# Sixteen instructions of batches 1 and 2 moved from VectorE to ScalarE in a fused attention + Fourier-mixing kernel

## The chip, the cores and the metric

The kernel runs on one core of a Trainium2 chip. The metric is the device time of one execution, in microseconds (us); lower is better. Engines are written as in the profile: PE is the matrix engine, PEld its weight loads, DVE is VectorE, ACT is ScalarE, POOL is GpSimd, SP issues most DMAs. L309 is line 309 of the kernel before.

## The reference

Four batches, each of 8 heads, 768 positions and 64 values per head. Stage one is block-sparse causal attention: a query sees its own block of 64 keys and the three blocks with the highest gate score (query times block mean of the keys). Stage two works on the 768 x 512 result `x` of each batch:

```python
mixed = real(fft(fft(x, axis=1), axis=2))
u = x + mixed
un = (u - mean(u)) / sqrt(var(u) + 1e-6)        # per row of 512
out = u + maximum(un @ w_ch1, 0) @ w_ch2        # 512 -> 2048 -> 512
```

## The kernel before, in words

Attention goes over 16 head pairs (`kk` = 0 to 15, four to a batch). For a pair, `stage_A` (L262) transposes k and q on PE into tiles `tp`; ACT casts the k parts to `kI` (L309), four casts to a pair, and DVE sums blocks into `kr` (L290). From pair 8 on, q is split into a high and a low half: ACT writes `qh` (L285) and DVE `ql` (L286). `stage_B` and `stage_C` compute gate scores and the mask, which DVE copies into `qg` (L355). `stage_S` (L374) makes scores `sc` in six sections to a pair; ACT's exp (L389) writes each to `ptl`, and from pair 7 on DVE masks the diagonal after the third section (L395). `stage_AV` (L397) multiplies with v into `av`, and DVE normalises into `x` (L415, L416).

A batch's Fourier part starts when its last pair is done:

- `stage_S1` (L463), twice (dt = 1, 0): sine sums `za` and cosine sums `ya` on PE. Each is evicted twice, in natural order (`zT`, `yT`, L487) and reversed (`zR`, `yR`, L489). DVE evicts z, ACT evicts y.
- `stage_S2` (L493), six row blocks (kt = 0 to 5): `mx` on PE, then `u` (L516) and row statistics (L518, L519) on DVE.
- `stage_N` (L523), once: a chain of small DVE instructions that ends in `rstd` and `nmr` (L543), then the normed rows `x`, six blocks: even ones on DVE (L546), odd ones on ACT (L550).
- `stage_T` (L553), six blocks: PE transposes a normed block into `unt` (L559), and it is evicted into `unT`: on DVE (L564), but the odd blocks of batch 0 on ACT (L562).
- `stage_M1` (L567), 16 units: `ha` and `hb` on PE (L575), ReLU to `hT` on ACT (L578) and DVE (L580). `stage_M2` (L583), 24 units of four matmuls (L589) into `ch`; after four units DVE adds `u` (L592) and SP stores.

The order on PE and POOL is written out by hand. The main loop (L713 to L747) emits attention of pair `kk`, and between its pieces `filler` takes units from a feed: `chain` holds the Fourier units of the batch just finished, `bulk` the M1 and M2 units of the batch before. A chain unit may go once a planned time (`feed.now`, costs of L597) has passed its predecessor by a gap (L603 to L605); until then bulk units go. So batch 1's Fourier part runs among batch 0's M2 units and the attention of pairs 8 to 10, and batch 2's among batch 1's M2 units and pairs 12 to 14. The order on the other engines is made by a scheduler; each engine runs its own list strictly in order.

Results of PE go to two pools: `sc` has 2 buffers (L380), everything else (`tp`, `av`, `mx`, `unt`, `ch`, `ha`, `hb`, `gt`, `za`, `ya`) shares 4 buffers of the tag `ps` (L152, L157). The scheduler picks which buffer a new tile takes, and the first matmul into it waits until the old tile's last reader is done.

Of the kernel before, what the change touches and what calls it, by code (L numbers as in the profile page):

```python
# [118 lines left out]
def kernel(  # L119
# [9 lines left out]
    nc = tc.nc  # L129
    B, H, S, D = q.shape  # L130
# [64 lines left out]


    LATE = 6


    SPLIT = 8  # L200
# [61 lines left out]
    def stage_A(kk, who, g):  # L262
# [18 lines left out]
        if who == 0:  # L281
            if kk < SPLIT:
                (nc.scalar.copy if kk == LATE else nc.vector.tensor_copy)(out=d["qt"][:, cols], in_=flat)
            else:
                nc.scalar.activation(out=d["qh"][:, cols], in_=flat, func=AF.Copy, scale=QS)  # L285
                STT(out=d["ql"][:, cols], in0=flat, scalar=QS, in1=d["qh"][:, cols], op0=MULT, op1=SUB)  # L286
            if g == 1 and kk != LATE:
                cast_q(kk)
# [174 lines left out]
    def stage_S1(b, dt):  # L463
        x = X[b]
        yps = pst([128, 2, KM], f"ya_{b}_{dt}")
        zps = pst([128, 2, KM], f"za_{b}_{dt}")


        if b == 0:
            zin, yin = ((ft[2], ft[0]), (ft[3], fc[1])) if dt == 1 else ((ft[2], fo[0]), (ft[3], ft[1]))  # L470
        else:
            zin, yin = (fo[dt],), (fc[dt],)
        for r in range(2):
            ops = [(x_[:, HST * r + t, :], ss_sb[:, t, r, :]) for x_ in zin for t in range(HST)]
            if dt == 0:
                ops += [(xmid[:, r, t, :], cs_sb[:, t, r, :]) for t in range(HST)]
            for n, (x_, w_) in enumerate(ops):
                nc.tensor.matmul(zps[:, r, :], x_, w_, start=(n == 0), stop=(n == len(ops) - 1))  # L478
        for r in range(2):
            ops = [(x_[:, HST * r + t, :], cs_sb[:, t, r, :]) for x_ in yin for t in range(HST)]  # L480
            for n, (x_, w_) in enumerate(ops):
                nc.tensor.matmul(yps[:, r, :], x_, w_, start=(n == 0), stop=(n == len(ops) - 1))
        for n, ps, cp in (("z", zps, nc.vector.tensor_copy), ("y", yps, nc.scalar.copy)):
            t0 = bpool.tile([128, KM, 2], F16, tag=f"{n}T", name=f"{n}T_{b}_{dt}", bufs=2)

            t1 = bpool.tile([128, KM - 1, 2], F16, tag=f"{n}R", name=f"{n}R_{b}_{dt}", bufs=2)
            cp(out=t0.rearrange("p m r -> p r m"), in_=ps)  # L487
            back = ps.rearrange("p r m -> p (r m)")[:, 1:KH - 1]
            cp(out=t1.rearrange("p m r -> p r m"),  # L489
               in_=back.rearrange("p (r m) -> p r m", r=2)[:, :, ::-1])  # L490
            x[n, dt] = (t0.rearrange("p m r -> p (m r)"), t1.rearrange("p m r -> p (m r)"))

    def stage_S2(b, kt):  # L493
        x = X[b]
        if kt == 0:
            x["u"] = bpool.tile([128, NST, DM], FP, tag="u_b", name=f"u_{b}", bufs=2)
            x["stat"] = spool.tile([128, NST, 2], FP, tag="stat6", name=f"stat6_{b}", bufs=2)
        u_b = x["u"]
        mps = pst([128, DM], f"mx_{b}_{kt}")
        hi = kt // HST  # L500
        ksl = slice(128 * (kt - HST * hi), 128 * (kt - HST * hi + 1))
        sd = sdp_sb if hi else sdn_sb
        for dt in range(2):
            half = mps[:, HD * dt:HD * (dt + 1)]
            nc.tensor.matmul(half, x["y", dt][hi][:, ksl], cd_sb[:, dt, :], start=(dt == 0), stop=False)  # L505
            nc.tensor.matmul(half, x["z", dt][hi][:, ksl], sd[:, dt, :], start=False,  # L506
                             stop=(dt == 1 and b > 0))
        split = dict(m=HD, r=2)
        xv = x["x"][:, kt, :].rearrange("p (m r) -> p m r", **split)
        uv = u_b[:, kt, :].rearrange("p (m r) -> p m r", **split)  # L510
        mv = mps.rearrange("p (r m) -> p m r", **split)
        if b == 0:
            nc.tensor.matmul(mps, id16, xv.rearrange("p m r -> p r m"), start=False, stop=True)
            nc.scalar.copy(out=uv, in_=mv)  # L514
        else:
            nc.vector.tensor_tensor(out=uv, in0=mv, in1=xv, op=ADD)  # L516
        bst = spool.tile([128, 6], FP, tag="bst", name=f"bst_{b}_{kt}")
        nc.vector.bn_stats(out=bst, in_=u_b[:, kt, :])  # L518
        nc.vector.bn_aggr(out=x["stat"][:, kt, :], in_=bst)  # L519
        if kt == NST - 1:  # L520
            stage_N(b)

    def stage_N(b):  # L523
        x = X[b]
        I32 = mybir.dt.int32
        stat = x["stat"]

        def small(n, dtype=FP):
            return spool.tile([128, NST], dtype, tag=n, name=f"{n}_{b}", bufs=2)

        rstd, nmr = small("rstd6"), small("nmr6")
        vr, yi, t2 = small("vr"), small("yi", I32), small("t2")
        ve = nc.vector
        ve.tensor_scalar(out=vr, in0=stat[:, :, 1], scalar1=1e-6, scalar2=None, op0=ADD)
        ve.tensor_scalar(out=yi, in0=vr.bitcast(I32), scalar1=1,
                         scalar2=None, op0=mybir.AluOpType.arith_shift_right)
        ve.tensor_scalar(out=yi, in0=yi, scalar1=-1, scalar2=0x5f3759df, op0=MULT, op1=ADD)
        y0 = yi.bitcast(FP)
        for _it in range(2):
            STT(out=t2, in0=y0, scalar=-0.5, in1=y0, op0=MULT, op1=MULT)  # L540
            ve.tensor_tensor(out=t2, in0=t2, in1=vr, op=MULT)
            STT(out=(rstd if _it == 1 else y0), in0=t2, scalar=1.5, in1=y0, op0=ADD, op1=MULT)
        STT(out=nmr, in0=stat[:, :, 0], scalar=-1.0, in1=rstd, op0=MULT, op1=MULT)  # L543
        for st in range(NST):
            if st % 2 == 0:
                nc.vector.tensor_scalar(out=x["x"][:, st, :], in0=x["u"][:, st, :],  # L546
                                        scalar1=stat[:, st, 0:1], scalar2=rstd[:, st:st + 1],
                                        op0=SUB, op1=MULT)
            else:
                nc.scalar.activation(out=x["x"][:, st, :], in_=x["u"][:, st, :], func=AF.Identity,  # L550
                                     scale=rstd[:, st:st + 1], bias=nmr[:, st:st + 1])

    def stage_T(b, st):  # L553
        x = X[b]
        if st == 0:
            x["unT"] = bpool.tile([128, NDT, S], F16, tag="unT", name=f"unT_{b}")
        tps = pst([128, NDT, 128], f"unt_{b}_{st}", dtype=F16)
        for dt in range(NDT):
            nc.tensor.transpose(tps[:, dt, :], x["x"][:, st, 128 * dt:128 * (dt + 1)], id16)  # L559
        dst = x["unT"][:, :, 128 * st:128 * (st + 1)]  # L560
        if b == 0 and st % 2 == 1:
            nc.scalar.copy(out=dst, in_=tps)  # L562
        else:
            nc.vector.tensor_copy(out=dst, in_=tps)  # L564
# [32 lines left out]
    M1_COST, M2_COST, S1_COST, S2_COST, T_COST = 1.3, 0.87, 1.3, 0.5, 0.43  # L597

    def queue_batch(b, start):
        last = start  # L600
        units = []

        s1_gap = 6.0 if b else 3.5  # L603
        s2_gap = 1.8 if 0 < b < B - 1 else 1.0
        t_gap = {0: 4.0, B - 1: 6.0}.get(b, 7.5)  # L605
        for dt in (1, 0):
            last = Unit(lambda dt=dt: stage_S1(b, dt), S1_COST, last, s1_gap if dt == 1 else 0.0)
            units.append(last)
        for kt in range(NST):
            last = Unit(lambda kt=kt: stage_S2(b, kt), S2_COST, last, 2.5 if kt == 0 else s2_gap)  # L610
            units.append(last)
        for st in range(NST):
            last = Unit(lambda st=st: stage_T(b, st), T_COST, last, t_gap if st == 0 else 0.2,
                        allowed=(lambda: b == 0 or m1_left[b - 1] == 0))
            units.append(last)

        def arm():
            def m1(it):
                stage_M1(b, it)
                m1_left[b] -= 1  # L620
            for it in range(NIT):
                feed.bulk.append(Unit(lambda it=it: m1(it), M1_COST))
            for st in range(NST):
                for part in range(4):
                    feed.bulk.append(Unit(lambda st=st, part=part: stage_M2(b, st, part), M2_COST))

        units.append(Unit(arm, 0.0, last, 0.8))
        feed.chain.extend(units)
# [19 lines left out]
    def main(fn, cost, *a):  # L648
        fn(*a)
        feed.spend(cost)  # L650
# [6 lines left out]
    with tc.manual_schedule(engines={mybir.EngineType.PE, mybir.EngineType.Pool}):  # L657
# [55 lines left out]
        for kk in range(NK):  # L713
            for p in range(6):
# [9 lines left out]
                if p == 2:  # L724
                    if kk + 2 < NK:
                        main(stage_AA, 0.7, kk + 2, 0)
                        if kk + 2 != LATE:
                            cast_v(kk + 2)
# [61 lines left out]
```

## Time and profile before

| | |
|---|---|
| median of 3 runs | 334.54 us (333.73 to 336.84) |
| profiled execution | 334.11 us, span 332.3 us, mean granted PE clock 0.99 |
| DVE busy | 236.8 us, 71% |
| ACT busy | 180.3 us, 54% |
| POOL busy | 83.8 us, 25% |
| ACT `x` L550, 128x512 (x12) | 804 ns each |
| DVE `x` L546, 128x512 (x12) | 542 ns each |
| ACT `unT` L562, 128x512 (x3) | 579 ns each |
| DVE `unT` L564, 128x512 (x21) | 419 ns each |
| ACT `yR` L489, 128x384 (x8) | 591 ns each |
| DVE `zR` L489, 128x384 (x8) | 572 ns each |

How to read it: all times come from one profiled execution, which took 334.11 us as a whole; the 1.81 us beyond the span lie around the program. A line of the timeline gives start, duration, engine, source line, operation, output<-input, shape, count, and in brackets the engine's idle time before it with what ended it. A row of several instructions is drawn from the first start to the last end, so neighbouring instructions overlap a little. PE records overlap as well (a 128x512 matmul is drawn with 379 ns, while 96 of them in a row take 20.73 us, 216 ns each), so what PE loses is read from the starts.

### The profile page before, as it was taken

To read this page: it belongs to the slowest core of one execution; us is meant where nothing else is said; L and a number is where in the kernel's file an instruction comes from. 1 tells how busy PE (TensorE), PEld (TensorE's weight loads), DVE (VectorE), ACT (ScalarE), POOL (GpSimd) and SP (SyncE) were. 2 spreads that over 40 slices of the span, in tenths; PEclk is the share of its full clock that TensorE was granted. 3 is DMA by queue.
4 is the path that set the end of the run, shared out by engine and by line. 5 is a ranking of instruction groups with operands and counts; after the bars stand their busy time and mean duration, and the time that the engine had idled before them with its cause. 6 is when DMAs were issued, how large, how long until landed. Compare 5 with 4: busy or idle time off the path is not lost.

```text
span 332.3 us, 7010 instructions
## 1 busy us (share of the span) xinstructions
PE 312.6 (94%) x2712; PEld 203.5 (61%) x2712; DVE 236.8 (71%) x750; ACT 180.3 (54%) x276; POOL 83.8 (25%) x137
## 2 busy tenths in 40 slices
PE   8799998995999989998999989999999999999995
PEld 3567776884766665565665666655666654556442
DVE  3877889689766898999666897998557588433211
ACT  3178889787876855438386854535764302244000
POOL 8545573452452030503132040502030000000000
PEclk9999999998799999999999999999999999999999
DMA  8999989995599341334424001010000011100021
GB/s 191 233 225 214 251 136 218 158 204 119 82 185 155 72 97 52 91 98 112 129 47 97 2 0 35 32 65 32 34 0 2 2 64 63 65 1 2 32 95 63
DMA packets 85312, 31.18 MB, mean 94 GB/s; under 512 B 77736, under 2 KB 81136, under 8 KB 85280
## 3 DMA queue, kind: packets, MB, share of 16 engines
q1 hardware_dynamic: 79984, 25.88, 31.2%
q0 software_dynamic: 3552, 4.40, 8.5%
q10 hardware_dynamic: 1744, 0.46, 0.6%
q8 instruction: 21, 0.34, 0.5%
q14 instruction: 11, 0.09, 0.1%
HBM read 28.63 MB, written 6.29 MB: 105 GB/s over the span
## 4 chain that ended last, share of the span: by engine, by line
PE 73%; DVE 16%; ACT 6%; DMA 1%; issue 1%; POOL 1%; ACTq 0%; DVEq 0%
PE ch L589 22%; PE ha L575 14%; PE sc L384 8%; PE hb L575 7%; PE av L410 5%; ACT kI L309 3%; PE g L321 3%; DVE mx L338 2%; PE za L478 2%; DVE ptl L395 2%; ACT ptl L389 2%; PE tp L277 2%; PE gt L352 2%; PE mx L505 2%; DVE kr L290 2%; PE mx L506 2%
## 5 line engine op out<-in xcount | busy, mean ns | idle before, releaser
L389 ACT ACTIVATE ptl<-sc 128x896 f16<-128x896 f32 x96 | 87.4, 918 | 46.5 <-PE sc L384 36.6
L589 PE MATMUL ch<-w_sb,hT 128*128 128x512 f16 x384 | 91.4, 379 | 0.5 <-DVE qT L286 0.5
L575 PEld LDWEIGHTS <-w_sb 128*128 128x128 f16 x512 | 48.8, 97 | 38.2 <-issue 4.3
L575 PE MATMUL ha<-unT,w_sb 128*128 128x512 f16 x256 | 65.7, 379 | 1.6 <-DVE hT L580 0.7
L384 PE MATMUL sc<-qg,kI 76*128 76x512 f16 (+3 forms) x256 | 55.7, 309 | 3.4 <-ACT ptl L389 3.4
L589 PEld LDWEIGHTS <-hT 128*128 128x128 f16 x384 | 36.2, 97 | 35.1 <-issue 0.6
L578 ACT ACTIVATE hT<-ha 128x512 f16<-128x512 f32 x64 | 38.1, 597 | 32.2 <-PE ha L575 32.1
L580 DVE TENSOR_SCALAR hT<-hb 128x256 f16<-128x256 f32 x64 | 26.8, 421 | 29.7 <-PE hb L575 29.5
L575 PE MATMUL hb<-unT,w_sb 128*128 128x256 f16 x256 | 38.4, 272 | 1.1 <-ACT hT L578 0.7
L427 POOL TENSOR_TENSOR fs<-x 128x384 f16<-128x384 f16 x12 | 10.9, 908 | 109.0 <-DVE x L416 88.5
L384 PEld LDWEIGHTS <-kI 76*128 76x128 f16 x256 | 24.2, 100 | 20.1 <-issue 3.1
L309 ACT CAST kI<-tp 64x384 f16<-64x384 f32 x57 | 27.0, 473 | 14.6 <-DVE kr L290 13.6
L592 DVE TENSOR_TENSOR u<-ch,u 128x512 f32<-128x512 f32 x24 | 16.5, 686 | 19.9 <-PE ch L589 19.6
L410 PE MATMUL av<-v,ptl 128*128 128x65 f16 x672 | 26.2, 195 | 0.0
L410 PEld LDWEIGHTS <-ptl 128*128 128x128 f16 x672 | 24.8, 98 | 1.9
L290 DVE TENSOR_REDUCE kr<-tp 128x6 f32<-128x384 f32 x32 | 17.2, 548 | 5.3 <-PE tp L277 5.3
L395 DVE TENSOR_TENSOR ptl<-ptl,ut 128x384 f16<-128x384 f16 x36 | 15.9, 479 | 6.0 <-ACT ptl L389 5.7
L550 ACT ACTIVATE x<-u,nmr,rstd 128x512 f16<-128x512 f32 x12 | 8.9, 804 | 19.0 <-DVE nmr L543 19.0
L388 PE MATMUL sc<-ltri,id 128*128 128x128 f16 x84 | 18.8, 224 | 0.0
L416 DVE TENSOR_TENSOR x<-av,rcp 128x384 f16<-128x384 f32 x32 | 17.8, 557 | 0.9
L518 DVE BATCH_NORM_STATS2 bst<-u 128x6 f32<-128x512 f32 x24 | 16.6, 692 | 1.2 <-ACT u L514 0.7
L355 DVE COPY qg<-gt 12x640 f16<-12x640 f16 x32 | 15.5, 484 | 1.8 <-PE gt L352 1.0
(112 smaller groups left out, 423.1 us busy)
## 6 DMA issues: line engine op xcount, KB each, us to landing
vn<-in_v_dram SPq DMA_DIRECT2D x32, 192.0 KB, 3.3
out_dram<-u SPq DMA_DIRECT2D x24, 256.0 KB, 2.0
kn<-in_k_dram SPq DMA_DIRECT2D x30, 192.0 KB, 3.5
qn<-in_q_dram SPq DMA_DIRECT2D x30, 192.0 KB, 3.4
w_sb<-in_moe_w_ch_dram POOLq DMA_DIRECT2D x8, 256.0 KB, 7.1
w_sb<-in_moe_w_ch_dram POOLq DMA_DIRECT2D x4, 512.0 KB, 8.2
cs_sb<-c_CS SPq DMA_DIRECT2D x1, 289.5 KB, 5.0
ss_sb<-c_SS SPq DMA_DIRECT2D x1, 289.5 KB, 5.3
```

The lines of the kernel that those rows point to most:

```text
L290: nc.vector.tensor_reduce(out=d["kr12"][:, 6 * g:6 * g + 6], in_=ps.rearrange("p a (x c) -> p a x c", x=2), axis=mybir.AxisListType.X, op=ADD)
L309: nc.scalar.copy(out=dst, in_=src_)
L384: nc.tensor.matmul(sp[:, co:co + (a1 - a0)], d["kI"][e][0:76, 128 * jt:128 * (jt + 1)], d["qg"][e][0:76, a0:a1], start=True, stop=not diag)
L388: nc.tensor.matmul(sp[:, co:co + 128], id16, ltri, start=False, stop=True)
L389: nc.scalar.activation(out=pt[:, SEC * s:SEC * (s + 1)], in_=sp[:, 0:SEC], func=AF.Exp, scale=0.125 if kk < SPLIT else 0.125 / QS)
L395: nc.vector.tensor_tensor(out=dg, in0=dg, in1=um, op=MULT)
L410: nc.tensor.matmul(av[:, st, 0:65], pt[:, o:o + 128], d["v16"][:, e, jt, 0:65], start=(cnt == 0), stop=(cnt == 20))
L416: nc.vector.tensor_tensor(out=x_b[:, :, 64 * h:64 * h + 64], in0=av[:, :, 0:64], in1=rcp.to_broadcast([128, NST, 64]), op=MULT)
L575: nc.tensor.matmul(hp_, w1_sb[:, dt, 128 * it:128 * (it + 1)], unT[:, dt, c0:c1], start=(dt == 0), stop=(dt == NDT - 1))
L578: nc.scalar.activation(out=hT[:, c0:c1], in_=hp_, func=AF.Relu)
L580: nc.vector.tensor_scalar(out=hT[:, c0:c1], in0=hp_, scalar1=0.0, scalar2=None, op0=mybir.AluOpType.max)
L589: nc.tensor.matmul(cps, x["hT"][it][:, 128 * st:128 * (st + 1)], w2_sb[:, it, :], start=(it == 0), stop=(it == NIT - 1))
```

## The change

A new name `BUSY` stands for batches 1 and 2. For these: the reversed casts `zR` go to ACT; all six normed blocks go to ACT; the odd `unT` evictions go to ACT. The gap before the first `stage_S2` unit is 3.5 in place of 2.5. Batches 0 and 3 are untouched (in batch 0 the odd `unT` evictions were on ACT already).

```diff
+    BUSY = range(1, B - 1)
...
-            cp(out=t1.rearrange("p m r -> p r m"),
+            (nc.scalar.copy if b in BUSY else cp)(out=t1.rearrange("p m r -> p r m"),
                in_=back.rearrange("p (r m) -> p r m", r=2)[:, :, ::-1])
...
         for st in range(NST):
-            if st % 2 == 0:
+            if st % 2 == 0 and b not in BUSY:
                 nc.vector.tensor_scalar(out=x["x"][:, st, :], in0=x["u"][:, st, :],
...
-        if b == 0 and st % 2 == 1:
+        if b < B - 1 and st % 2 == 1:
             nc.scalar.copy(out=dst, in_=tps)
...
-        s2_gap = 1.8 if 0 < b < B - 1 else 1.0
+        s2_gap = 1.8 if b in BUSY else 1.0
...
-            last = Unit(lambda kt=kt: stage_S2(b, kt), S2_COST, last, 2.5 if kt == 0 else s2_gap)
+            last = Unit(lambda kt=kt: stage_S2(b, kt), S2_COST, last, (3.5 if b in BUSY else 2.5) if kt == 0 else s2_gap)
```

In the built programs the lists of POOL are the same. ACT has 16 instructions more, DVE 16 fewer. On PE one thing moves: in batch 2, one unit of four `ch` matmuls stands ahead of the first `mx` unit in place of behind it. On SP one output store and one load of q change places. What PE's matmuls wait for changes around the transposes, since the scheduler hands out the `ps` buffers differently.

## The prediction

> **What bounds the kernel now.** I read the busy table first, then what PE waited for, then the timeline of all engines around the two places where the normed blocks are made, and last the granted clock around PE's one long stall.
>
> ```profile
> PE 312.6 (94%) x2712; PEld 203.5 (61%) x2712; DVE 236.8 (71%) x750; ACT 180.3 (54%) x276; POOL 83.8 (25%) x137
> ```
>
> PE is the bound, with 312.6 of 332.3 us. So an instruction moved between DVE and ACT is worth only what it takes from, or adds to, PE's waits. Counted from the starts of PE's instructions (each start against the usual step behind such an instruction), PE loses about 7 us in all between 119 and 262 us, where the Fourier parts of batches 1 and 2 lie. Most of it has causes that the change doesn't touch (0.8 at 119.20 and 1.2 at 196.43 behind ReLUs of DVE, 0.35 at 175.26). The waits near the change are these:
>
> ```profile
> PE unt L559 <- DVE x L416: 0.7, 1, 0.7
> ...
> PE ch L589 <- DVE qT L286: 0.5, 1, 0.5
> ```
>
> Both lie in batch 1's normed blocks. From the starts they cost PE 0.84 and 0.69 us. With the 0.49 us that the fourth `mx` of batch 1 waited at 138.20 for DVE's L286, 2.0 us is all that a lighter DVE could give back.
>
> The timeline of batch 1, of ACT, DVE and PE:
>
> ```profile
> 150.28 1.46 DVE L546 TENSOR_SCALAR x<-u,stat,rstd 128x512 f16<-128x512 f32 x3
> 150.43 2.22 ACT L550 ACTIVATE x<-u,nmr,rstd 128x512 f16<-128x512 f32 x3
> ...
> 152.67 1.46 ACT L309 CAST kI<-tp 64x384 f16<-64x384 f32 x3
> ...
> 153.20 0.38 PE L559 MATMUL unt<-id,x 128*128 128x128 f16 x4 [0.67 <-DVE x L416]
> ...
> 154.15 1.73 ACT L389 ACTIVATE ptl<-sc 128x896 f16<-128x896 f32 x2
> ...
> 155.76 0.55 PE L384 MATMUL sc<-qg,kI 76*128 76x512 f16 x3
> ...
> 157.06 1.02 PE L589 MATMUL ch<-w_sb,hT 128*128 128x512 f16 x4 [0.53 <-DVE qT L286]
> ```
>
> ACT works here without a pause: norms, casts, exps, each starting as the one before ends. In the program the first `unt` takes the buffer of a `tp` whose reader is the first of those casts, which ends near 153.15; the L416 that the bracket names ends at nearly the same time. PE already waits for ACT's list, not for DVE's sum. Batch 2:
>
> ```profile
> 224.46 2.22 ACT L550 ACTIVATE x<-u,nmr,rstd 128x512 f16<-128x512 f32 x3 [0.54 <-DVE nmr L543]
> ...
> 226.59 0.90 ACT L389 ACTIVATE ptl<-sc 128x896 f16<-128x896 f32 x1
> ...
> 228.03 0.92 ACT L389 ACTIVATE ptl<-sc 128x896 f16<-128x896 f32 x1 [0.55 <-PE sc L384]
> ...
> 230.00 0.55 PE L384 MATMUL sc<-qg,kI 76*128 76x512 f16 x3
> ```
>
> Here no casts of k stand in the list, ACT has pauses, and PE loses nothing.
>
> **The change part by part.** In all DVE is freed of 4 x 0.572 + 6 x 0.542 + 6 x 0.419 = 8.1 us, and ACT takes 4 x 0.591 + 6 x 0.804 + 6 x 0.579 = 10.7 us. Neither is on the path by itself.
>
> *Reversed casts, 4.* ACT's casts there start 0.45 us apart (122.19, 122.65). In batch 1 the second new cast stands ahead of the exp at 125.61, which so starts 0.45 later. DVE sat idle for 1.30 us until 126.57, waiting for that exp: the 1.1 us it was freed of go into that idle, and its mask starts 0.45 later. It then works on without idle to 135.15, where 0.28 of idle absorb that much. About 0.2 us reach the L286 that `mx` waits for at 138.20. Cost 0.2; bounds 0 (an idle I don't see) and 0.9 (both casts in full). In batch 2 the exp at 201.97 is 0.1 later, DVE again only idles (1.41 us before 202.91), and no PE wait follows it. Nothing; without that cover 0.45.
>
> *Gap of 3.5.* One unit of four `ch` matmuls (0.86 us) changes places with one `mx` unit in batch 2. The work is the same, and PE lost nothing there. Nothing; if the first `mx` were now the late one, its 0.43 us. The SP swap is two issues of about 0.4 us, of a q that pair 14 needs far later. Nothing.
>
> *Normed blocks and evictions, batch 1.* Six blocks on ACT: three take 2.22, one 0.80, so each further one 0.71; the six end at 150.43 + 0.80 + 5 x 0.71 = 154.78 instead of 152.65. Everything behind them on ACT is 2.13 later. Queued there are three casts to `kI`, two exps, two L285, an exp. Now PE, step by step:
> - First `unt`: takes the buffer of `av`, freed by L416, which DVE reaches earlier without its blocks (near 152.45). Starts near 152.5 in place of 153.20: 0.7 won.
> - Second `unt` waits for the eviction of the first (0.42 on DVE): 153.4. Then `ch`, 0.86.
> - q transposes take the buffer of the cast that now ends at 155.27: start 155.3, before 154.88.
> - Third `unt` takes the buffer of the last cast, 154.78 + 1.46 = 156.26: 156.3, before 155.54.
> - Score section at 155.76 needs the first exp's buffer: 156.28 + 0.92 = 157.20. Start 157.25, 1.5 later.
> - The `ch` of 157.06 takes the buffer of the second `unt`, which ACT evicts behind both exps: 156.28 + 1.73 + 0.58 = 158.6. 1.5 later.
> - ACT's L285, behind that eviction, then DVE's L286: the `gt` and `unt` at 158.01 and 158.41 go near 159.7 and 160.2.
>
> From there ACT has pauses (2.63 us before 160.09, 2.05 before 163.06), and the remaining `unT` fit in them. PE stays 1.75 us late. Bounds: 1.1, if L285 and L286 follow closer than I laid them; 2.1, the whole delay of ACT. I take 1.75, since the exp and the eviction alone make 1.5.
>
> *Batch 2.* The six end at 224.46 + 4.35 = 228.8, the two exps at 229.8 and 230.7. The score section of 230.00 finds its buffer free by 0.2. The sixth `unt` (232.57) waits for an eviction on ACT that stands behind one more exp: 230.7 + 0.58 + 0.9 + 0.58 = 232.8. Cost 0.3; bounds 0 and 1.75 (batch 1's). DVE's freed 1.45 us meet no PE wait.
>
> Sum: 0.2 + 1.75 + 0.3 = 2.25 us, on the profiled execution's 334.11: 336.4. That execution is 0.43 under the median of its three runs, so the sum is a little low if the next runs lie like that median.
>
> *The clock.* PE's granted clock fell once in this trace:
>
> ```profile
> 78.00:80.00 2.00, 0.43 (x5) 0.24 (x3) 1.90 (x6) 1.61 (x3) 1.23 (x2) 1.00 0.48 110
> 80.00:82.00 2.00, 0.52 (x4) 0.34 (x4) 1.93 (x6) 0.94 (x2) 0.54 (x1) 0.59 0.82 186
> ```
>
> (PE busy, PEld, DVE, ACT, POOL, clock.) PE was idle from 78.43 to 81.48; the clock went to half at 80.37, after 1.94 us of that idle, and stayed there for 6.83 us. By the same grid of 3.41 us, the stretch before the fall held 23% of matmul time (by starts, 216 ns to 512 columns), and the emptiest ones that kept their clock about 50%. My waits in batch 1 leave the idlest 3.41 us with some 44%, most of it transposes. So the row allows a fall without showing one: 0 to 3.4 us (half of 6.83). I take 0, since 44 is nearer to 50 than to 23. The Trainium skill ("TensorE: Matmul & The Clock Gate", rules for kernel authors) asks for no idle gaps over about 3 us between bursts; by it gaps of 0.3 to 0.9 us cost nothing and the sum stands. The trace is stricter, since the clock fell with 1.94 us of the gap behind it.
>
> **The rivals.**
> - *A lighter DVE pays (faster, or not slower).* PE's waits at 138.20, 153.20 and 157.06 vanish and ACT's list doesn't reach PE: 334.1 - 2.0 = 332.1, or with only part of it up to 334.8. For it: DVE is over 90% busy in 140 to 160, ACT 54% over all. Against: ACT has no pause from 150.06 to 157.46, and the exps wait behind the norms. It decides if the casts and exps that PE needs stand ahead of the added blocks; in the built list they stand behind.
> - *Batch 2 goes like batch 1.* If the score section of 230.00 misses its 0.2 us of margin and the waits chain, 1.75 in place of 0.3: 337.8. For it: the margin is small. Against: no casts there.
> - *The clock falls in batch 1.* 336.4 + 3.4 = 339.8. For it: the idle pieces lie close together. Against: no single one is over 0.9 us.
> - That the change does nothing at all would be 334.1, and falls under the first.
>
> **How the numbers follow.** Chances: the sum 0.56, with a range of its own of 335.0 to 337.4 (bounds of batch 1, and 0.3 to either side for the rest); DVE pays 0.16; batch 2 like batch 1 0.14; clock 0.14. A measurement of this kernel can tell about 1% from no change, 3.3 us: faster is under 331.2, slower over 337.9. Faster: 0.03, the far end of the first rival. Slower: the clock's 0.14, half of batch 2's, and a tail of the sum: 0.25. Same: 0.72. The range goes from 333.6 (upper half of the first rival) to 339.0 (batch 2 in full, and a part of a clock loss), and leaves out some 2 in 10.
>
> **What would show it.** After: six L550 in a row of about 4.35 us in each batch; the L309 and L389 behind them in batch 1 later by 2.1; PE waits of L277, L559, L384 and L589 between 153 and 160 us on ACT, 3 us in all, in place of 1.5; almost none in batch 2; the mask after batch 1's casts 0.45 later, its DVE idle longer. I am wrong if PE waits less around batch 1's transposes than before, if the six blocks take less than 4 us, or if the clock row has a second fall.

## The result and the profile after

The changed kernel takes 336.54 us (median of 18 runs, 335.81 to 339.18) against 334.43 us for the kernel before (18 runs, 333.29 to 336.86): ratio 1.0066, 95% interval 1.0049 to 1.0083, so about 2.2 us slower, under what counts as a difference here. The prediction was 336.4 us. The profiled execution took 336.49 us, its span is 334.7 us (before: 334.11 and 332.3).

In some executions of any of these kernels (7 of 12 of e11_first_cast and 4 of 10 of e3_unt, but 2 of 17 and 4 of 31 of the kernel before beside them) PE's mean granted clock is lower by 0.005 or more, as one more stretch of 3.41 us at half clock makes it, and the time is some 1.7 us longer, so effects of a few tenths are read below from marks in the profiled executions and not from medians.

The busy row of the page after:

```profile
PE 313.5 (94%) x2712; PEld 203.4 (61%) x2712; DVE 229.0 (68%) x734; ACT 188.9 (56%) x292; POOL 83.8 (25%) x137
```

DVE lost 16 instructions and 7.8 us, ACT gained 16 and 8.6 us (the prediction laid 8.1 and 10.7 us from the durations of single instructions, which overlap when they stand in a row), and PE has the same instructions. What PE waits for (waits in us, times, longest):

```profile
PE sc L386 <- ACT ptl L391: 3.8, 7, 0.8
...
PE tp L279 <- ACT kI L311: 0.9, 2, 0.5
...
PE ch L592 <- ACT unT L565: 0.5, 1, 0.5
```

The two rows that the prediction shows of before named DVE (x L416, qT L286), and they are gone. The first two rows above are mostly waits elsewhere that the kernel before has too:

```profile
PE sc L384 <- ACT ptl L389: 3.4, 6, 0.8
...
PE tp L277 <- ACT kI L309: 0.4, 1, 0.4
```

New are one wait for an exp, one for the casts to `kI`, and the one for an eviction. (Line numbers of the changed kernel are 2 higher, from L489 on 3 higher: L309 is now L311, L389 is L391, L559 is L562, L562 is L565, L589 is L592. In the experiments they differ again by a few; the names of the tiles stay.)

The timeline of batch 1's normed blocks, ACT and PE:

```profile
151.12 4.34 ACT L553 ACTIVATE x<-u,nmr,rstd 128x512 f16<-128x512 f32 x6
...
153.32 0.38 PE L562 MATMUL unt<-id,x 128*128 128x128 f16 x4
...
155.48 1.46 ACT L311 CAST kI<-tp 64x384 f16<-64x384 f32 x3
...
156.01 0.88 PE L279 MATMUL tp<-id,qn 128*128 128x128 f32 x6 [0.55 <-ACT kI L311]
...
156.96 1.73 ACT L391 ACTIVATE ptl<-sc 128x896 f16<-128x896 f32 x2
...
157.94 0.56 PE L386 MATMUL sc<-qg,kI 76*128 76x512 f16 x3 [0.56 <-ACT ptl L391]
...
158.57 0.59 ACT L565 COPY unT<-unt 128x512 f16<-128x512 f16 x1
...
159.22 1.02 PE L592 MATMUL ch<-w_sb,hT 128*128 128x512 f16 x4 [0.50 <-ACT unT L565]
```

ACT has one unbroken list: six blocks, three casts, two exps, then the eviction, each starting as the one before ends. Each of PE's three brackets ends as the first of a group on that list ends. Counted from the starts, PE lost 0.84 and 0.69 us here before and 1.56 us more now, about 3.1 in all. Batch 2:

```profile
227.21 4.35 ACT L553 ACTIVATE x<-u,nmr,rstd 128x512 f16<-128x512 f32 x6 [1.04 <-DVE nmr L546]
...
231.46 1.70 ACT L391 ACTIVATE ptl<-sc 128x896 f16<-128x896 f32 x2
...
232.41 0.55 PE L386 MATMUL sc<-qg,kI 76*128 76x512 f16 x3
```

The score section starts as the first of the two exps ends; PE lost 0.16 us there.

Marks: PE's order is the same in nearly all places, so the start of the same PE instruction can be compared in two traces. The last three columns of the table say by how many us a kernel falls behind the kernel before in each of three stretches: S1 is batch 1's first `za` to its last `mx`, N1 its last `mx` to its first `ha`, N2 the same of batch 2. Between and behind these nothing moves by more than 0.02.

| kernel | median, us (runs) | ratio, 95% interval | S1 | N1 | N2 |
|---|---|---|---|---|---|
| changed | 336.54 (18) | 1.0066 (1.0049 to 1.0083) | 0.43 | 1.56 | 0.17 |
| e1_casts | 335.08 (10) | 1.0034 (0.9999 to 1.0069) | 0.42 | 0 | 0 |
| e2_norms | 335.58 (10) | 1.0036 (1.0015 to 1.0058) | 0 | 1.12 | 0 |
| e3_unt | 334.83 (10) | 1.0036 (1.0007 to 1.0065) | 0 | -0.14 | 0 |
| e4_no_dve_blocks | 334.42 (10) | 1.0008 (0.9976 to 1.0039) | 0 | -0.01 | 0 |
| e5_jit | 335.37 (12) | 1.0031 (1.0006 to 1.0056) | 0.44 | 0.21 | 0.13 |
| e6_jit_split | 333.65 (12) | 0.9983 (0.9958 to 1.0009) | 0 | 0.09 | 0 |
| e7_b2_only | 334.11 (12) | 0.998 (0.9949 to 1.0011) | 0 | 0 | 0.16 |
| e8_nine | 340.6 (6) | 1.0187 (1.0142 to 1.0231) | 0.43 | 5.63 | 0.16 |
| e9_opposite | 336.53 (6) | 1.0069 (1.0048 to 1.009) | 0 | 2.74 | 0 |
| e10_no_evict | 336.31 (6) | 1.0066 (1.004 to 1.0091) | 0.43 | 1.10 | 0.15 |
| e11_first_cast | 335.74 (12) | 1.0031 (1.0004 to 1.0058) | 0 | 0 | 0 |
| e12_gap | 336.33 (12) | 1.0049 (1.0027 to 1.0071) | 0.42 | 1.55 | 0 |

The changed kernel's marks sum to 2.16; its span grew by 2.4. The other 0.26 is there before the first changed instruction: the first `za` of batch 1 starts at 121.24 instead of 120.98. It differs from run to run (0.61 early in e6_jit_split) and, as it lies ahead of all that was changed, is no part of the change.

### The profile page after: what moved, and what is told of

The parts are those of the page before. It is cut to its first block, busy times and chain, and to the rows that moved or that the text cites. A ratio compares the mean times of both kernels' runs of the same rounds, so it can differ in the third digit from the quotient of the medians.

```text
span 334.7 us, 7009 instructions
## 1 busy us (share of the span) xinstructions
PE 313.5 (94%) x2712; PEld 203.4 (61%) x2712; DVE 229.0 (68%) x734; ACT 188.9 (56%) x292; POOL 83.8 (25%) x137
## 4 chain that ended last, share of the span: by engine, by line
PE 72%; DVE 17%; ACT 8%; issue 1%; POOL 1%; DVEq 0%; ACTq 0%
PE ch L592 20%; PE ha L578 14%; PE sc L386 8%; PE hb L578 7%; PE av L412 5%; ACT kI L311 4%; PE g L323 3%; ACT ptl L391 2%; DVE mx L340 2%; PE za L480 2%; DVE ptl L397 2%; PE warm L365 2%; DVE kr L292 2%; PE gt L354 2%; PE tp L279 2%; PE ya L484 1%
## 5 line engine op out<-in xcount | busy, mean ns | idle before, releaser
L391 ACT ACTIVATE ptl<-sc 128x896 f16<-128x896 f32 x96 | 87.4, 920 | 40.0 <-PE sc L386 29.6
L592 PE MATMUL ch<-w_sb,hT 128*128 128x512 f16 x384 | 91.4, 379 | 0.5 <-ACT unT L565 0.5
L592 PEld LDWEIGHTS <-hT 128*128 128x128 f16 x384 | 36.2, 98 | 35.1 <-issue 0.6
L311 ACT CAST kI<-tp 64x384 f16<-64x384 f32 x57 | 27.1, 475 | 15.2 <-DVE kr L292 14.2
L553 ACT ACTIVATE x<-u,nmr,rstd 128x512 f16<-128x512 f32 x18 | 13.2, 806 | 19.5 <-DVE nmr L546 19.5
L240 POOL COPY qg<-qT 64x768 f16<-64x768 f16 x16 | 13.7, 858 | 13.6 <-ACT qT L287 13.2
```

The lines of the kernel that those rows point to most:

```text
L311: nc.scalar.copy(out=dst, in_=src_)
L391: nc.scalar.activation(out=pt[:, SEC * s:SEC * (s + 1)], in_=sp[:, 0:SEC], func=AF.Exp, scale=0.125 if kk < SPLIT else 0.125 / QS)
L592: nc.tensor.matmul(cps, x["hT"][it][:, 128 * st:128 * (st + 1)], w2_sb[:, it, :], start=(it == 0), stop=(it == NIT - 1))
```

## The experiments

Theory: what PE pays is set by what stands ahead of the casts and exps in ACT's list, in the order it has there. Rivals: the amount of work on ACT or DVE sets it; a lighter DVE pays something back; the clock takes part.

**One part alone: casts, normed blocks, evictions, and DVE lightened without ACT.**

e1_casts, the kernel before with

```diff
-            cp(out=t1.rearrange("p m r -> p r m"),
+            (nc.scalar.copy if b in (1, 2) else cp)(out=t1.rearrange("p m r -> p r m"),
```

> Before, with only the reversed sine casts of batches 1 and 2 on ScalarE. My theory (the exp behind the second cast starts 0.45 us late, the mask and all of DVE's list behind it too, and batch 1's mx waits longer): PE is 0.4 us later by the third mx group of batch 1, nothing in batch 2, 334.8 in all. Rival, a lighter DVE pays: the mx of batch 1 waits less than the 0.49 us of before, 334.0 or less. Rival, ACT's added time counts in full: 4 x 0.45 = 1.8 us, 336.2.

Measured: 0.42 in S1, nothing elsewhere. Before, ACT's exp and DVE's mask behind it:

```profile
125.61 0.93 ACT L389 ACTIVATE ptl<-sc 128x896 f16<-128x896 f32 x1
...
126.57 0.63 DVE L395 TENSOR_TENSOR ptl<-ptl,ut 128x384 f16<-128x384 f16 x2 [1.30 <-ACT ptl L389]
```

In e1_casts (start, duration, engine, line, then the idle time before it and its cause):

```profile
124.82 0.58 ACT L489 CAST zR<-za 128x384 f16<-128x384 f32 x1
...
125.69 0.94 ACT L389 ACTIVATE ptl<-sc 128x896 f16<-128x896 f32 x1
...
126.67 0.63 DVE L395 TENSOR_TENSOR ptl<-ptl,ut 128x384 f16<-128x384 f16 x2 [2.21 <-ACT ptl L389]
```

This trace runs 0.35 earlier at that place (its first `mx` is at 127.77, before at 128.12), so exp and mask are 0.44 late; DVE's idle before the mask grew to 2.21. What DVE does after it is late too: `kr`, and behind it the casts to `kI`, for which `av` waits 0.23. At L286 `mx` waits 0.16 more, as the two masks ahead of L286 took longer. Before:

```profile
135.76 1.33 DVE L395 TENSOR_TENSOR ptl<-ptl,ut 128x384 f16<-128x384 f16 x2
```

In e1_casts:

```profile
135.67 1.49 DVE L395 TENSOR_TENSOR ptl<-ptl,ut 128x384 f16<-128x384 f16 x2
```

The six kernels that have the second cast of batch 1 on ACT show 1.49 or 1.50 us there, the other eight 1.33. POOL is busy beside these masks all the time in both traces; why they took 0.16 longer isn't shown.

e11_first_cast, the same for dt = 1 alone (`if b in (1, 2) and dt == 1`):

> The kernel before with only the first of the two reversed sine casts of batches 1 and 2 on ACT. Both casts on ACT cost 0.42 us in batch 1, by way of an exp that starts 0.44 later behind the second one, a mask of DVE behind that exp, and what DVE does after it. Theory: the first cast delays an exp that nobody waits for, and ACT has 0.68 us of idle before its next cast; cost 0. Rival (each cast on ACT costs its share): 0.2.

Measured: 0 at every mark. So the place of the second cast costs 0.42, and the first, as long, costs nothing.

e2_norms, the kernel before with

```diff
-            if st % 2 == 0:
+            if st % 2 == 0 and b not in (1, 2):
```

> Before, with all normed blocks of batches 1 and 2 on ScalarE and nothing else moved. My theory (three more blocks of 0.71 us stand ahead of the casts and exps that PE waits for): PE loses 1.4 to 1.7 us in batch 1 between the last mx and the first ha, 0 to 0.2 in batch 2; 336.0. Rival, it is the evictions behind the exps that cost: 0.5 or less here, 334.9. Rival, a lighter DVE pays: 0.8 us won in batch 1, 333.6.

Measured: 1.12 in N1, 0 in N2: the mechanism, at less than expected. The score section carries it:

```profile
155.88 1.73 ACT L389 ACTIVATE ptl<-sc 128x896 f16<-128x896 f32 x2
...
156.86 0.55 PE L384 MATMUL sc<-qg,kI 76*128 76x512 f16 x3 [1.16 <-ACT ptl L389]
```

e3_unt, the kernel before with

```diff
-        if b == 0 and st % 2 == 1:
+        if b < B - 1 and st % 2 == 1:
```

> Before, with only the odd transpose evictions of batches 1 and 2 on ScalarE. My theory: each stands behind one exp, but without the three added blocks ACT is 2.1 us earlier, so PE waits only where the buffer of the second transpose is taken, at most 0.3 us more in batch 1 and none in batch 2; 334.4 to 334.8. Rival, the evictions carry half of the loss: 335.5. Rival, a lighter DVE pays: 333.9 or less.

Measured: -0.14 in N1, 0 in N2. By themselves the evictions cost nothing.

e4_no_dve_blocks, the kernel before, in which the even normed blocks of batches 1 and 2 are left out (the rows stay unnormed):

```diff
         for st in range(NST):
+            if st % 2 == 0 and b in (1, 2):
+                continue
```

> Before, with the even normed blocks of batches 1 and 2 left out altogether: the rows stay unnormed, so DVE is freed of 3.2 us at the spot and ACT is given nothing. It measures what a lighter DVE alone can give. My theory (PE waits there for ACT's casts, behind ACT's own three blocks): the first transpose of batch 1 starts no earlier against av than in before, less 0.1; 0.0 to 0.4 us won in all, 334.2. Rival, a lighter DVE pays: the waits at the first transpose (0.84) and at the ch behind L286 (0.69) go, 333.0.

Measured: -0.01 in N1, 0 in N2, though DVE was rid of six blocks and ACT got none. The first `unt` comes 0.66 sooner, and PE loses it again a little later:

```profile
155.00 1.73 ACT L389 ACTIVATE ptl<-sc 128x896 f16<-128x896 f32 x2
...
156.76 0.63 DVE L395 TENSOR_TENSOR ptl<-ptl,ut 128x384 f16<-128x384 f16 x2 [0.74 <-ACT ptl L389]
...
157.30 1.01 DVE L286 SCALAR_TENSOR_TENSOR qT<-tp,qT 128x384 f16<-128x384 f32 x2
...
157.91 1.02 PE L591 MATMUL ch<-w_sb,hT 128*128 128x512 f16 x4 [1.13 <-DVE qT L286]
```

That L286 follows DVE's mask, and the mask waits 0.74 us for the second of ACT's exps. ACT's exps stand behind the same casts and start where they did before (154.15, in a trace that is 0.86 earlier here). A lighter DVE gives nothing back here.

**What the parts do together.** The single parts give 0.42 + 1.12 - 0.14 = 1.40, the whole 2.16.

e10_no_evict, the changed kernel with

```diff
-        if b < B - 1 and st % 2 == 1:
+        if b == 0 and st % 2 == 1:
```

> The changed kernel with all evictions of batches 1 and 2's norm transposes on DVE, so casts and normed blocks on ACT alone. The single parts add up to 1.40 us, the whole to 2.16. Theory: the 0.44 and 0.17 us that are missing come from evictions that stand behind late exps in ACT's list, so without them batch 1's norms cost what they cost alone (1.1 to 1.2), casts 0.43, batch 2 nothing: 334.1 + 1.6 = 335.7. Rival (the missing part comes from casts and norms together): batch 1 1.5 and batch 2 0.17, as in the changed kernel, 336.3.

Measured: 0.43, 1.10, 0.15. In N1 the theory holds: without evictions the normed blocks cost what they cost alone, so 0.46 comes from evictions that stand behind late exps (the `ch` at 159.22 above). In N2 it fails: the 0.15 is there without evictions.

e7_b2_only, the changed kernel with `BUSY = range(2, B - 1)`, batch 1 as before:

> The changed kernel with batch 1 as in the kernel before; batch 2 alone has the reversed casts, six normed blocks and odd evictions on ACT, and the gap of 3.5. Theory (a cover, not the amount, sets the price; in batch 2 no casts to kI stand behind the blocks and ACT has pauses): 0 to 0.2 us in batch 2, 334.3. Rival (each batch pays for what is put on ACT): half of the 2.2 us, 335.2.

Measured: 0.16 in N2, 0 in N1. ACT's work in batch 2, as much as in batch 1, costs a tenth of it.

e12_gap, the changed kernel with

```diff
-            last = Unit(..., last, (3.5 if b in BUSY else 2.5) if kt == 0 else s2_gap)
+            last = Unit(..., last, 2.5 if kt == 0 else s2_gap)
```

> The changed kernel with the gap before the first mx unit back at 2.5, so that PE's order in batch 2 is the one of the kernel before (the unit of four ch matmuls behind the first mx again). The runs with the gap of 3.5 lose 0.15 to 0.17 us in batch 2 (at the score section that waits for an exp); the single parts, with the gap of 2.5, lose nothing there. Theory (the gap: it moves DVE's work so that nmr and with it the six blocks come some 0.5 later against PE): the 0.16 is gone and batch 2 costs 0.00; the rest of the changed kernel's loss stays, 2.0 in all. Rival (casts and normed blocks together make it): batch 2 still costs 0.15 to 0.17.

Measured: N2 is 0, S1 and N1 stay. The same places as in batch 2 above:

```profile
226.63 4.34 ACT L553 ACTIVATE x<-u,nmr,rstd 128x512 f16<-128x512 f32 x6 [0.53 <-DVE nmr L546]
...
230.88 1.69 ACT L391 ACTIVATE ptl<-sc 128x896 f16<-128x896 f32 x2
...
232.17 0.55 PE L386 MATMUL sc<-qg,kI 76*128 76x512 f16 x3
```

The six blocks start 2.77 before the first `unt` (229.40) instead of 2.27 (229.48 in the changed kernel), the first exp ends near 231.8, and the section at 232.17 finds its buffer. The gap of 3.5 had made `nmr` 0.5 late and used up the margin. It costs so together with six blocks on ACT; the gap alone, on the kernel before, wasn't run.

**Place against amount.**

e5_jit, the changed kernel with blocks made just in time in batches 1 and 2:

```diff
-        for st in range(NST):
+        for st in range(2 if b in (1, 2) else NST):
+            norm_block(b, st)
...
+        if b in (1, 2) and st + 2 < NST:
+            norm_block(b, st + 2)
```

(`norm_block` is the old loop body; the second addition stands in `stage_T`, ahead of its transposes.)

> The changed kernel with one thing altered: in batches 1 and 2 only the normed blocks 0 and 1 are made at once; block st+2 is made just before the transposes of block st. The same instructions run on the same engines; only their order in ACT's list changes (in batch 1: two normed blocks, the three casts to kI, exp, block, exp, block, eviction, and so on), so the casts and exps that PE waits for stand behind two blocks and no longer behind six. Theory (the place in ACT's list decides, not the amount of work on ACT): between the last mx and the first ha of batch 1 the changed kernel lost 1.56 us on the kernel before; here it loses 0.5 or less. The casts' 0.43 us and batch 2's 0 to 0.2 stay. Sum 334.1 + 0.4 + 0.4 = 334.9, about 1.6 under the changed kernel. Rival (amount: ACT carries 5.3 us more in batch 1 and PE must pay for it wherever it stands): still 1.5 late there, 336.4.

Measured: N1 0.21 instead of 1.56, with the same instructions on the same engines.

```profile
151.23 1.52 ACT L559 ACTIVATE x<-u,nmr,rstd 128x512 f16<-128x512 f32 x2
...
152.76 1.46 ACT L311 CAST kI<-tp 64x384 f16<-64x384 f32 x3
...
157.71 0.38 PE L570 MATMUL unt<-id,x 128*128 128x128 f16 x4 [1.02 <-DVE unT L575]
```

The casts now follow two blocks, and the score section (156.15) waits for nothing. What is left is the fourth `unt`, for an eviction of DVE that stands behind a mask, behind the second exp.

e6_jit_split, the kernel before with the same order and its own split:

> The kernel before with the same just-in-time order in batches 1 and 2 and nothing else: even normed blocks on DVE and odd ones on ACT as before, but ACT makes one block ahead of the casts to kI instead of three. Theory (place in ACT's list): PE's waits of 0.84 us (first unt) and 0.69 us (ch behind L286) in the kernel before are also waits for ACT's list; they go in part, 0.5 to 1.3 us, to about 333.2. Rival (those waits are DVE's, or the buffers'): no difference, 334.1; or a loss where a transpose now waits for a block made too late, up to 0.5.

Measured: 0.09 in N1. The first `unt`'s 0.84 is gone, but not won: the fourth `unt` now waits 1.38, as the second exp (153.65) stands behind a block, and behind that exp DVE's mask and add.

```profile
152.94 0.80 ACT L556 ACTIVATE x<-u,nmr,rstd 128x512 f16<-128x512 f32 x1
...
154.59 0.84 DVE L395 TENSOR_TENSOR ptl<-ptl,ut 128x384 f16<-128x384 f16 x2 [0.85 <-ACT ptl L389]
...
156.08 0.38 PE L567 MATMUL unt<-id,x 128*128 128x128 f16 x4 [1.22 <-DVE u L600]
```

e9_opposite, e6_jit_split with one block moved the other way:

```diff
-        if st % 2 == 0:
+        if st % 2 == 0 or (b == 1 and st == 3):
```

> The kernel before with the just-in-time order of the run before last in batches 1 and 2, and in batch 1 the fourth normed block moved the other way, from ACT to DVE (four blocks on DVE, two on ACT). In the just-in-time kernel the fourth transpose waited 1.38 us for DVE's add of u, which stood behind the mask, behind the second exp, behind that block on ACT. Theory (ACT's list is the chain): the second exp starts 0.6 us earlier, that wait shrinks by 0.2 to 0.7, and batch 1 gains 0.2 to 0.7 us on the kernel before: about 333.7. Rival (by now DVE's own list is the chain, 0.54 us longer): no gain, the wait moves to the evictions of the first transposes, 334.1.

Measured: 2.74 in N1; both theory and rival fell short.

```profile
152.93 0.80 ACT L556 ACTIVATE x<-u,nmr,rstd 128x512 f16<-128x512 f32 x1
...
153.64 0.91 ACT L389 ACTIVATE ptl<-sc 128x896 f16<-128x896 f32 x1
...
154.48 0.91 POOL L428 TENSOR_TENSOR fs<-x 128x384 f16<-128x384 f16 x1
...
154.58 1.92 DVE L395 TENSOR_TENSOR ptl<-ptl,ut 128x384 f16<-128x384 f16 x2 [0.39 <-ACT ptl L389]
...
155.37 1.82 POOL L238 COPY qg<-qT 64x768 f16<-64x768 f16 x2
...
157.15 0.38 PE L567 MATMUL unt<-id,x 128*128 128x128 f16 x4 [2.07 <-DVE u L600]
```

The scheduler put the sixth block into the place of the fourth, so the second exp started no sooner (153.64). The mask, with POOL busy beside it all the time, took 1.92 instead of 0.84. PE so waited 2.23, which put it 1.07 behind e6_jit_split, and then the clock fell (below), which accounts for the other 1.58. As the exp did not move, this run doesn't test what an earlier exp would give. No version beats the kernel before.

**More of the suspected wait.** e8_nine, the changed kernel with the odd blocks of batch 1 written twice:

```diff
+                if b == 1 and st % 2 == 1:
+                    nc.scalar.activation(out=x["x"][:, st, :], in_=x["u"][:, st, :], func=AF.Identity,
+                                         scale=rstd[:, st:st + 1], bias=nmr[:, st:st + 1])
```

> The changed kernel with the three odd normed blocks of batch 1 written twice by ACT, nine instead of six in a row: 2.13 us more of ACT ahead of the casts and exps. Theory: the whole 2.13 us reaches PE in batch 1, since ACT's list already bounds PE there: 336.5 + 2.1 = 338.6, clock unchanged. Rival 1 (other work covers part): under 1 us more, 337.4. Rival 2 (the granted clock): with longer waits the emptiest 3.41 us in batch 1 hold less than the 42% that kept the clock in the changed kernel; if the clock falls to half there, up to 3.4 us on top, 342.

Measured: N1 5.63, 4.07 more than in the changed kernel. The score section again waits for the first exp:

```profile
160.56 1.73 ACT L391 ACTIVATE ptl<-sc 128x896 f16<-128x896 f32 x2
...
161.53 0.93 PE L386 MATMUL sc<-qg,kI 76*128 76x512 f16 x3 [0.36 <-ACT ptl L391]
```

The exps start at 160.56 instead of 156.96, and this trace was 1.47 late before: 2.13 later, the theory's whole amount. The other 1.94 is the clock's, as busy times by stretches show (start and end of a stretch, length, then busy time of PE, PEld, DVE, ACT, POOL, the granted clock, DMA share, GB/s). The clock changes only at times that lie 3.41 us apart; the stretches are cut there. The changed kernel:

```profile
155.70:159.11 3.41, 2.04 (x17) 1.44 (x18) 1.31 (x4) 3.35 (x7) 0.00 (x0) 1.00 0.52 144
```

e8_nine:

```profile
156.95:160.36 3.41, 1.09 (x6) 0.69 (x7) 0.69 (x1) 3.36 (x6) 0.00 (x0) 1.00 0.20 77
160.36:163.77 3.41, 2.83 (x14) 1.58 (x14) 1.63 (x5) 3.39 (x7) 0.17 (x1) 0.50 0.51 115
163.77:167.19 3.42, 3.42 (x16) 1.48 (x15) 1.83 (x4) 1.06 (x2) 2.29 (x3) 0.50 0.00 0
```

e9_opposite:

```profile
154.72:158.13 3.41, 1.26 (x10) 0.73 (x9) 3.41 (x6) 1.39 (x3) 3.23 (x4) 1.00 0.30 72
158.13:161.54 3.41, 3.41 (x16) 1.49 (x15) 1.95 (x5) 0.00 (x0) 0.00 (x0) 0.50 0.97 238
```

With 2.04 us of PE in the emptiest stretch the clock stayed (in the next it is 1.00 still); behind a stretch with 1.09 or 1.26 it was at half for two stretches or one.

## Why the prediction was right

The time (336.4 against 336.54) and the mechanism of batch 1 held. Each of the four terms was off by 0.17 to 0.30, two of them up and two down, so that the sum came so near is partly luck.

- **"PE already waits for ACT's list, not for DVE's sum."** Shown: by e4_no_dve_blocks (DVE lighter, nothing won), e8_nine (2.13 us more on ACT, 2.13 later) and e5_jit (other order, 1.35 of 1.56 gone). For the first `unt` by itself it isn't shown: in e4_no_dve_blocks it started 0.66 sooner, behind DVE's L416 and ahead of the cast's end. But nothing came of that, as PE met ACT's list a little later.
- **Batch 1's steps.** Less the 0.69 by which this trace is late before them (0.26 from run to run, 0.43 from the casts), PE's starts are: first `unt` 152.63 (predicted 152.5), second 153.52 (153.4), q transposes 155.32 (155.3), third `unt` 156.30 (156.3), score section 157.25 (157.25), `ch` 158.53 (158.6), `gt` 159.52 (159.7), `unt` 159.98 (160.2). The term was 1.75, measured 1.56: L285 and L286 followed closer than laid, as the lower bound had it.
- **Reversed casts: 0.2 predicted, 0.43 measured,** within the bounds of 0 to 0.9. The 0.45 on exp and mask was right (0.44). The step "0.28 of idle absorb that much. About 0.2 us reach the L286" left out another way: DVE's late `kr` makes the casts to `kI` late, and `av` waits 0.23 for them. So PE itself was 0.27 late at 135.15, and DVE's idle there shrank only from 0.28 to 0.10. The other 0.16 reached L286 not from the late exp as laid but from two masks that took 1.49 in place of 1.33.
- **Gap of 3.5: "Nothing" predicted, 0.17 measured.** The step looked for an idle PE at the place where the unit moved. The cost came 27 us later: `nmr` is 0.5 late, and the score section of batch 2 misses its margin (e12_gap).
- **Batch 2: 0.3 predicted, 0 measured** for the six blocks and evictions (e12_gap). The sixth `unt` didn't wait. The bound at 1.75 was far off; ACT's list there holds no casts to `kI` and has pauses.
- The terms so are 0.43 + 1.56 + 0.17 + 0 = 2.16 against 2.25; the errors cancelled for the most part.
- **A lighter DVE pays:** fell by e4_no_dve_blocks. The rival's argument was that DVE is over 90% busy there. The Trainium skill ("Perfetto Trace Analysis", Optimizing Scalar/DVE Operations) says that with DVE saturated, moving some work to ScalarE may make sense; in this case it cost 1.56 us in batch 1, as ACT, 56% busy over all, had no pause at that place.
- **The clock falls in batch 1:** it didn't, at 42% of matmul time in the emptiest stretch. It was near: in e8_nine, with 2.13 us more of waits, it fell. The Trainium skill ("TensorE: Matmul & The Clock Gate", What's actually happening) has the clock drop after at least one idle window of about 3.4 us. In e8_nine the longest pause of PE that touches the stretch was 1.14 us; the measurement decides, and a stretch need not be empty.

## What to carry to other kernels

Before work is moved to an engine with a low busy share, write out that engine's list at the very place, and ask what PE needs from behind the new instructions; three more blocks (2.13 us) cost 1.12 us ahead of the casts of batch 1 and nothing in batch 2, where ACT had pauses, and the whole change in another order cost 0.21 instead of 1.56 at batch 1's blocks and evictions. What the other engine is freed of counts only if PE waits for that engine, and a wait that names it may itself stand behind the first. A margin of 0.2 us can be eaten by a small edit more than 20 us earlier, so follow a moved unit to the next place where a chain starts from it.

## What the runs showed of the hardware

- The clock falls behind a stretch of its 3.41 us grid that is only partly empty. By matmul time counted from the starts (216 ns to 512 columns, and twice that for float32, whose 128 columns start 0.11 us apart in the transposes of q), stretches with 19% (e8_nine), 23% (before), 27% (e9_opposite), 33% (e2_norms, 76.35 to 79.76) and 36% (e8_nine, 13.59 to 17.00) lost it, 40% (e4_no_dve_blocks, 13.21 to 16.63) and 42% (the changed kernel) kept it. The shares are estimates from the starts in the traces; the edge between 36% and 40% wasn't looked for.
- Two masks of DVE (f16, two inputs of 128x384) took 0.63 us with POOL idle (the changed kernel, 158.72). With POOL adding and copying beside them the whole time they took 1.33 (before, 135.76), 1.49 (e1_casts, 135.67) and 1.92 us (e9_opposite, 154.58); what in POOL's work sets the amount wasn't tested. No step of the prediction had a price for that.
